# Chunks of 64 tokens in an mLSTM cell with a multiplicative FFN: cell products on 64x64 quarters of TensorE, with loads, gates and schedule rearranged to suit

## The chip, the cores and the metric

The kernel runs on one core of a Trainium2 chip. The metric is the device time of one execution in microseconds. Each kernel was executed at least four times and profiled once. Where a run was slow (over 1.5% above the fastest of its kernel) the ratios leave it out. The inputs and outputs are fp32, except for the FFN weights, which arrive as 64-bit floats and are converted on the chip.

## The reference

```python
# attention: batch 4, heads 8, tokens 768, head size 40
for t in range(S):
    m_new  = max(f[t] + m, i[t]);  f_s = exp(f[t] + m - m_new);  i_s = exp(i[t] - m_new);  m = m_new
    C = f_s * C + i_s * outer(v[t], k[t]);   n = f_s * n + i_s * k[t]
    y[t] = sigmoid(o[t]) * (C @ q[t]) / max(|n . q[t]|, 1)
# FFN on x = y reshaped to (3072 tokens, 320)
out = ((x @ w1) * (x @ w2)) @ w3 @ w_out          # d_ff = 1024
```

The recurrence is computed in chunks. Within a chunk a masked and weighted score matrix replaces the loop. Between chunks a state carries C and n. The kernel folds w3 @ w_out into one matrix (w3o) on the chip.

## The kernel before

A chunk is 128 tokens, and a unit is one chunk of one batch: 24 units. Each step of the main loop brings one unit through its stages, with pieces of FFN work in between, so that TensorE has something to do while other engines work for the cell. A cell has four products: ss (scores), ph (weighted scores times v), pi (state times q) and pc (what is added to the state). An FFN "up" makes 128 hidden columns for 512 tokens, a "down" the output of 128 tokens, and the "fold" is w3 @ w_out. The gate row of every head is written to DRAM once and read back into all 128 partitions (`pw`), exponentiated by ScalarE and masked by GpSimd.

```python
L = 128                                   # tokens of a chunk
def load_u(n):                            # the gate rows of unit n, in every partition
    u_t[n] = io.tile([L, H, L], FP, name="pw", tag="pw", bufs=4)
    nc.sync.dma_start(out=u_t[n], in_=U_d[c][b * H:(b + 1) * H, :].unsqueeze(0).to_broadcast([L, H, L]))
def scores(n):                            # two heads at once, in two halves of the rows
    for p in range(NP):
        for hip in range(2):
            r = slice(hip * DP, (hip + 1) * DP)
            nc.tensor.matmul(ss[hip][:, p, :], lhsT=kT[r, p, :], rhs=qT[r, p, :], start=True, stop=True)
    ...                                   # pw = ss * pw, on VectorE
def cell(n):
    ...   # pi: state times q, 4 matmuls of 82 columns;  h = pi * gT
    for hd in range(H):
        nc.tensor.matmul(ph[:, hd, :], lhsT=pw[:, hd, :], rhs=vt[:, hd, :], start=True, stop=True)   # 41 columns
    ...   # h += ph;  pc: k times weighted v, 4 matmuls of 82 columns;  state += pc
def ffn_up(gr, f):                        # pa, pb: 2 full products each, then the 64 remaining rows of both, side by side
    ...
```

Of the kernel before, what the change touches and what calls it, by code (L numbers as in the profile page):

```python
# [8 lines left out]
FP = mybir.dt.float32  # L9
# [6 lines left out]
def kernel(  # L16
# [27 lines left out]
    L = 128  # L44
    NT = S // L
    NU = B * NT
# [4 lines left out]
    BH = B * H  # L51
    DFF = moe_w1.shape[1]
    FO = DFF // L
    KF = DM // L
    REM = DM - KF * L
    GT = B
    TG = GT * L
# [16 lines left out]


    NB, NBQ = 4, 3
    qbuf = [const.tile([L, H, DP], FP, name=f"qbuf{i}") for i in range(NBQ)]
    kbuf = [const.tile([L, H, DP], FP, name=f"kbuf{i}") for i in range(NB)]
    vbuf = [const.tile([L, H, D1], FP, name=f"vbuf{i}") for i in range(NB)]
    ident = const.tile([128, 128], FP, name="ident")  # L80
    one = const.tile([BH, 1], FP, name="one")
    state = [const.tile([128, NP, 2, D1], FP, name=f"state{b}") for b in range(B)]
    aT = const.tile([L, NT, BH], FP, name="aT")
    gT = const.tile([L, NT, BH], FP, name="gT")
    wT = const.tile([L, NT, BH], FP, name="wT")
    decP = const.tile([128, B * NP, NT], FP, name="decP")
    U_d = [dram.tile([BH, L], FP, name=f"U_d{c}") for c in range(NT)]
# [3 lines left out]

    def load(n):
        c, b = divmod(n, B)
        for dst, src in ((qbuf[n % NBQ][:, :, 0:D], q), (kbuf[n % NB][:, :, 0:D], k), (vbuf[n % NB][:, :, 0:D], v)):
            nc.sync.dma_start(out=dst, in_=src[b, :, c * L:(c + 1) * L, :].rearrange("h p d -> p h d"))

    def load_o(c):
        o_t[c] = io.tile([L, B, H, D], FP, name="o_in", tag="o_in", bufs=2)
        for b in range(B):
            nc.sync.dma_start(out=o_t[c][:, b], in_=o_gate[b, :, c * L:(c + 1) * L, :].rearrange("h p d -> p h d"))  # L100

    def load_u(n):
        c, b = divmod(n, B)
        u_t[n] = io.tile([L, H, L], FP, name="pw", tag="pw", bufs=4)
        nc.sync.dma_start(out=u_t[n], in_=U_d[c][b * H:(b + 1) * H, :].unsqueeze(0).to_broadcast([L, H, L]))


    with tc.tile_pool(name="gates", bufs=1) as gates:
        f_sb = gates.tile([BH, S], FP, name="f_sb")
        a = gates.tile([BH, S], FP, name="a")  # L110
        nc.sync.dma_start(out=f_sb, in_=f_gate.rearrange("b h s -> (b h) s"))
        nc.sync.dma_start(out=a, in_=i_gate.rearrange("b h s -> (b h) s"))
        load(0)

        nc.vector.memset(one, 1.0)
        make_identity(nc, ident)
        for i in range(NB):
            nc.gpsimd.memset(kbuf[i][:, :, D:DP], 0.0)
            if i < NBQ:
                nc.gpsimd.memset(qbuf[i][:, :, D:DP], 0.0)  # L120
            nc.gpsimd.memset(vbuf[i][:, :, D:D1], 1.0)
        for t in state:
            nc.gpsimd.memset(t, 0.0)

        F = gates.tile([BH, S], FP, name="F")
        U = gates.tile([BH, S], FP, name="U")
        g, w = F, f_sb
        m0 = gates.tile([BH, NT], FP, name="m0")
        dec = gates.tile([BH, NT], FP, name="dec")

        def gate_cols(src, dst, c0, c1):
            pg = tps([L, c1 - c0, BH], "pg")
            for c in range(c0, c1):
                nc.tensor.transpose(pg[:, c - c0, :], src[:, c * L:(c + 1) * L], ident[0:BH, 0:BH])
            nc.vector.tensor_copy(out=dst[:, c0:c1, :], in_=pg)


        nc.vector.tensor_copy(out=f_sb[:, 0:1], in_=a[:, 0:1])
        for c0, c1 in ((0, 1), (1, NT)):
            rs = slice(c0 * L, c1 * L)  # L140
            for c in range(c0, c1):
                r = slice(c * L, (c + 1) * L)
                nc.vector.tensor_tensor_scan(out=F[:, r], data0=one.to_broadcast([BH, L]), data1=f_sb[:, r], initial=0.0,
                                             op0=OP.mult, op1=OP.add)
                if c > 0:
                    nc.vector.tensor_scalar(out=a[:, r], in0=a[:, r], scalar1=m0[:, c:c + 1], scalar2=None,
                                            op0=OP.subtract)
                nc.vector.tensor_tensor_scan(out=U[:, r], data0=f_sb[:, r], data1=a[:, r],
                                             initial=0.0 if c else -1.0e30, op0=OP.add, op1=OP.max)
                if c == 0:  # L150
                    nc.vector.tensor_copy(out=m0[:, 1:2], in_=U[:, L - 1:L])
                elif c < NT - 1:
                    nc.vector.tensor_tensor(out=m0[:, c + 1:c + 2], in0=m0[:, c:c + 1],
                                            in1=U[:, (c + 1) * L - 1:(c + 1) * L], op=OP.add)
            nc.vector.tensor_tensor(out=U[:, rs], in0=F[:, rs], in1=U[:, rs], op=OP.subtract)
            for c in range(c0, c1):
                nc.sync.dma_start(out=U_d[c], in_=U[:, c * L:(c + 1) * L])
            nc.vector.tensor_tensor(out=a[:, rs], in0=a[:, rs], in1=F[:, rs], op=OP.subtract)
            gate_cols(a, aT, c0, c1)
            if c0 == 0:  # L160
                for n in range(2):
                    load_u(n)
                load_o(0)
                load(1)
            U3, w3d, a3 = (x.rearrange("p (c t) -> p c t", t=L)[:, c0:c1] for x in (U, w, a))
            nc.vector.tensor_tensor(out=w3d, in0=a3, in1=U3[:, :, L - 1:L].to_broadcast([BH, c1 - c0, L]), op=OP.add)
            nc.scalar.activation(out=dec[:, c0:c1], in_=U3[:, :, L - 1], func=AF.Exp)
            nc.scalar.activation(out=g[:, rs], in_=U[:, rs], func=AF.Exp)
            nc.scalar.activation(out=w[:, rs], in_=w[:, rs], func=AF.Exp)
            gate_cols(w, wT, c0, c1)  # L170
            if c0 > 0:
                gate_cols(g, gT, c0, c1)


        nc.sync.dma_start(out=dec_d, in_=dec)
        for hip in range(2):
            nc.sync.dma_start(out=decP[hip * DP:(hip + 1) * DP],
                              in_=dec_d.rearrange("(n two) c -> two n c", two=2)[hip:hip + 1]
                              .to_broadcast([DP, B * NP, NT]))

    ffn = ctx.enter_context(tc.tile_pool(name="ffn", bufs=2))
# [7 lines left out]
    w3_t = {}  # L189
# [3 lines left out]
    def to_f32(dst, pieces):  # L193
# [3 lines left out]
        raw = wst.tile([128, n, 2], U32, name="raw", tag="raw", bufs=2)  # L197
        for rows, src in pieces:
            nc.sync.dma_start(out=raw[rows].rearrange("p n two -> p (n two)"), in_=src)
# [16 lines left out]
    every = slice(0, 128)  # L216

    def cvt_w12(half, i):
        c0 = half * CW
        if i < 2 * KF:  # L220
            dst, src = ((w1, w1_d), (w2, w2_d))[i // KF]
            ko = i % KF
            to_f32(dst[:, ko, c0:c0 + CW], [(every, src[ko * 128:(ko + 1) * 128, cols(c0, CW)])])
        else:
            to_f32(wr[:, c0:c0 + CW], [(slice(j * REM, (j + 1) * REM), src[KF * L:DM, cols(c0, CW)])
                                       for j, src in enumerate((w1_d, w2_d))])

    def cvt_wo(ko):
        to_f32(wo[:, ko, :], [(every, wo_d[ko * 128:(ko + 1) * 128, :])])

    def cvt_w3(ko):
        w3_t[ko] = wst.tile([128, DFF], FP, name="w3", tag="w3")
        for c0 in range(0, DFF, CW):
            to_f32(w3_t[ko][:, c0:c0 + CW], [(every, w3_d[ko * 128:(ko + 1) * 128, cols(c0, CW)])])
# [4 lines left out]
    def w3_trans(ko):  # L239
        w3 = w3_t.pop(ko)  # L240
        w3T_t[ko] = wst.tile([128, FO, 128], FP, name="w3T", tag="w3T")
        for half in range(2):
            tp = tps([128, FO // 2, 128], "w3p")
            for j in range(FO // 2):
                ki = half * (FO // 2) + j
                nc.tensor.transpose(tp[:, j, :], w3[:, ki * 128:(ki + 1) * 128], ident)
            r = slice(half * (FO // 2), (half + 1) * (FO // 2))
            if half:
                nc.scalar.copy(out=w3T_t[ko][:, r, :], in_=tp)
            else:  # L250
                nc.vector.tensor_copy(out=w3T_t[ko][:, r, :], in_=tp)  # L251
# [11 lines left out]
    def out_gate(c):  # L263
        nc.scalar.activation(out=o_t[c], in_=o_t[c], func=AF.Sigmoid)
# [194 lines left out]
```

## Time and profile before

| | before |
|---|---|
| median of 4 runs | 578.04 us (572.49 to 580.81) |
| span of the profiled run | 573.4 us |
| TensorE busy | 532.6 us, 93% |
| units arrive in steps 0 to 5 | every 5 to 13 us |
| step 20 (two ups, one down, a unit's whole cell) | 19.3 us |

The prediction below shows the shares, the stages and a unit's chain.

### The profile page before, as it was taken

Reading aid. Unit: us, or ns where it says so; the run is one execution under the profiler, and the core shown is the slowest. Engines: PE = TensorE matmul, PEld = TensorE weight load, DVE = VectorE, ACT = ScalarE, POOL = GpSimd, SP = SyncE. Lnnn points to the kernel's source line nnn. Section 1 sums busy time; section 2 is a strip of 40 time slices with the busy share of each in tenths; the row PEclk is TensorE's granted clock in tenths of the full one; section 3 lists DMA queues with packets and bytes.
Section 4 is the critical chain, followed back from the end, with each engine's and each line's share of the span. In section 5 each row is a group of like instructions: output and inputs, shape, how many; then the busy total and the mean of one; then the engine's idle time right before and its main releaser. Section 6 shows DMA issues by size and latency. Waiting matters only on the chain.

```text
span 573.4 us, 6858 instructions
## 1 busy us (share of the span) xinstructions
PE 532.6 (93%) x2521; PEld 339.2 (59%) x2521; DVE 256.7 (45%) x581; ACT 166.2 (29%) x377; POOL 72.6 (13%) x105
## 2 busy tenths in 40 slices
PE   0869899889698999999999999999999999999997
PEld 0759766546366566688886656565453353535375
DVE  7356989997978665765431332132001101010100
ACT  2745354534231314434553211111111111111100
POOL 2222322142011202122220100000000000000000
PEclk9985799989798998999999999999999999999999
DMA  7499986868353554334733200000000000000010
GB/s 163 71 202 225 212 185 156 181 164 201 97 170 111 144 127 114 97 72 108 152 95 95 59 13 11 13 7 5 23 24 1 0 24 0 23 1 23 0 35 34
DMA packets 114224, 49.28 MB, mean 86 GB/s; under 512 B 103440, under 2 KB 106704, under 8 KB 114192
## 3 DMA queue, kind: packets, MB, share of 16 engines
q1 hardware_dynamic: 114192, 48.85, 36.3%
q8 instruction: 20, 0.33, 0.2%
q14 instruction: 12, 0.10, 0.1%
HBM read 44.81 MB, written 4.03 MB: 85 GB/s over the span
## 4 chain that ended last, share of the span: by engine, by line
PE 78%; DVE 13%; DMA 4%; ACT 2%; SPq 1%; issue 1%; ACTq 0%; DVEq 0%
PE po L375 18%; PE pa L364 12%; PE pb L364 12%; PE pa L367 7%; PE wp L257 7%; PE ph L309 6%; PE pt L278 4%; PE ss L289 4%; PE pc L320 3%; PE pi L304 3%; DMA kbuf<-in_k_dram 2%; DMA raw<-in_moe_w_dram 2%; DVE pw L292 2%; DVE ex L208 2%; PE px L351 1%; DVE ma L210 1%
## 5 line engine op out<-in xcount | busy, mean ns | idle before, releaser
L370 DVE TENSOR_TENSOR ab<-pb,a_sb 128x512 f32<-128x512 f32 x48 | 33.2, 691 | 212.8 <-ACT a_sb L369 212.6
L375 PE MATMUL po<-w3o,ab 128*128 128x320 f32 x384 | 105.9, 433 | 0.0
L364 PE MATMUL pa<-xT,w 128*128 128x512 f32 x192 | 93.9, 610 | 0.5 <-ACT xT L352 0.5
L364 PE MATMUL pb<-xT,w 128*128 128x512 f32 x192 | 91.3, 597 | 0.0
L375 PEld LDWEIGHTS po<-w3o,ab 128*128 128x128 f32 x384 | 71.9, 190 | 31.4 <-issue 3.0
L369 ACT COPY a_sb<-pa 128x512 f32<-128x512 f32 x48 | 28.1, 585 | 187.4 <-PE pb L367 187.4
L270 ACT ACTIVATE pw<-pw,aT 128x128 f32<-128x128 f32 x192 | 60.1, 391 | 24.7 <-DMA pw<-U_d 24.6
L364 PEld LDWEIGHTS pb<-xT,w 128*128 128x128 f32 x192 | 36.6, 192 | 45.0 <-issue 44.7
L364 PEld LDWEIGHTS pa<-xT,w 128*128 128x128 f32 x192 | 33.2, 191 | 37.3 <-issue 34.9
L367 PE MATMUL pa<-xT,wr 64*128 64x512 f32 x96 | 53.9, 641 | 0.1
L367 PE MATMUL pb<-xT,wr 64*128 64x512 f32 x96 | 53.9, 641 | 0.0
L309 PE MATMUL ph<-vbuf,pw 128*128 128x41 f32 x384 | 50.9, 292 | 1.9 <-DVE pw L292 1.0
L309 PEld LDWEIGHTS ph<-vbuf,pw 128*128 128x128 f32 x384 | 48.8, 203 | 3.7 <-DVE pw L292 1.3
L257 PE MATMUL wp<-wo,w3T 128*128 128x320 f32 x128 | 40.8, 475 | 5.6 <-DVE w3T L251 5.5
L271 POOL TENSOR_SCALAR_AFFINE_SELECT pw<-pw 128x1024 f32<-128x1024 f32 x24 | 31.6, 1316 | 104.4 <-ACT pw L270 103.6
L292 DVE TENSOR_TENSOR pw<-ss,pw 128x512 f32<-128x512 f32 x48 | 30.9, 682 | 11.2 <-PE ss L289 11.1
L257 PEld LDWEIGHTS wp<-wo,w3T 128*128 128x128 f32 x128 | 26.0, 209 | 16.5 <-DVE w3T L251 6.2
L367 PEld LDWEIGHTS pa<-xT,wr 64*128 64x128 f32 x96 | 14.1, 184 | 36.5 <-issue 35.5
L289 PEld LDWEIGHTS ss<-qT,kT 64*128 64x128 f32 x384 | 28.2, 210 | 10.1 <-issue 6.2
L378 ACT COPY o_sb<-po 128x320 f32<-128x320 f32 x24 | 10.2, 425 | 78.3 <-PE po L375 75.5
L289 PE MATMUL ss<-qT,kT 64*128 64x128 f32 x384 | 30.9, 303 | 1.4 <-ACT qT L281 1.1
L320 PE MATMUL pc<-vw,kbuf 128*128 128x82 f32 x160 | 24.6, 302 | 0.1
(75 smaller groups left out, 520.3 us busy)
## 6 DMA issues: line engine op xcount, KB each, us to landing
pw<-U_d SPq DMA_DIRECT2D x24, 512.0 KB, 5.2
raw<-in_moe_w_dram SPq DMA_DIRECT2D x24, 512.0 KB, 4.0
qbuf<-in_q_dram SPq DMA_DIRECT2D x24, 160.0 KB, 4.2
kbuf<-in_k_dram SPq DMA_DIRECT2D x24, 160.0 KB, 3.9
vbuf<-in_v_dram SPq DMA_DIRECT2D x24, 160.0 KB, 3.9
o_in<-in_o_gate_dram SPq DMA_DIRECT2D x24, 160.0 KB, 3.8
out_dram<-o_sb SPq DMA_DIRECT2D x24, 160.0 KB, 1.8
raw<-in_moe_w_out_dram SPq DMA_DIRECT2D x8, 320.0 KB, 3.2
```

Source lines behind the costliest of these rows:

```text
L257: nc.tensor.matmul(wp, lhsT=w3T[:, ki, :], rhs=wo[:, ki, :], start=(ki == 0), stop=(ki == FO - 1))
L270: nc.scalar.activation(out=pw[:, h, :], in_=pw[:, h, :], func=AF.Exp, bias=aT[:, c, b * H + h:b * H + h + 1])
L271: nc.gpsimd.affine_select(out=pw, in_=pw, compare_op=OP.is_ge, fill=0.0, base=0, pattern=[[0, H], [1, L]], channel_multiplier=-1)
L289: nc.tensor.matmul(ss[hip][:, p, :], lhsT=kT[r, p, :], rhs=qT[r, p, :], start=True, stop=True)
L292: nc.vector.tensor_tensor(out=pv[:, :, hip, :], in0=ss[hip], in1=pv[:, :, hip, :], op=OP.mult)
L309: nc.tensor.matmul(ph[:, hd, :], lhsT=pw[:, hd, :], rhs=vt[:, hd, :], start=True, stop=True)
L320: nc.tensor.matmul(pc[:, p].rearrange("p a b -> p (a b)"), lhsT=kbuf[n % NB][:, 2 * p:2 * p + 2, :].rearrange("p a b -> p (a b)"), rhs=vw[ ...
L364: nc.tensor.matmul(p, lhsT=wt[:, cc, fs], rhs=x[:, cc, :], start=(cc == 0), stop=False)
L367: nc.tensor.matmul(p, lhsT=wr[r, fs], rhs=x[r, KF, :], start=False, stop=True)
L369: nc.scalar.copy(out=a_sb, in_=pa)
L370: nc.vector.tensor_tensor(out=ab_t[gr][:, f, :], in0=pb, in1=a_sb, op=OP.mult)
L375: nc.tensor.matmul(po, lhsT=ab_t[gr][:, f, j * L:(j + 1) * L], rhs=w3o[:, f, :], start=(f == 0), stop=(f == FO - 1))
```

## The change

The chunk becomes 64 tokens. A unit is now the same 64 tokens of two batches, so that it still fills 128 partitions. All cell products become matmuls of 64 rows by 64 columns, addressed to the four quarters of the array, four at a time (two for `ph`). The first weights are fetched right after the gate inputs. The gates of all later chunks are computed in one pass. FFN work starts two steps earlier, conversions go two pieces a step. The q, k, v and o loads become two half-unit transfers each, since the halves come from different batches.

```diff
-    L = 128
+    L = 64
...
     def load_u(n):
-        u_t[n] = io.tile([L, H, L], FP, name="pw", tag="pw", bufs=4)
-        nc.sync.dma_start(out=u_t[n], in_=U_d[c][b * H:(b + 1) * H, :].unsqueeze(0).to_broadcast([L, H, L]))
+        u_t[n] = io.tile([P, H, L], FP, name="pw", tag="pw", bufs=3)
+        src = (U_rest[c - 1] if c else U_first).rearrange("(two bp h) t -> bp two (h t)", two=2, bp=NB2)[bp]
+        nc.sync.dma_start(out=u_t[n].rearrange("p h t -> p (h t)"), in_=src.unsqueeze(1).to_broadcast([2, L, H * L]))
...
     def scores(n):
-            for hip in range(2):
-                r = slice(hip * DP, (hip + 1) * DP)
-                nc.tensor.matmul(ss[hip][:, p, :], lhsT=kT[r, p, :], rhs=qT[r, p, :], start=True, stop=True)
+            for hip, x in ((0, 0), (1, 1), (0, 1), (1, 0)):
+                r, t = halves[hip], halves[x]
+                nc.tensor.matmul(ss[t, hip, p, :], lhsT=kT[r, p, t], rhs=qT[r, p, t], start=True, stop=True)
...
     def cell(n):            # pi and pc likewise in four quarters, ph in the two diagonal ones
+            for r in halves:
+                nc.tensor.matmul(ph[r, hd, :], lhsT=pw[r, hd, :], rhs=vt[r, hd, :], start=True, stop=True)
...
-    n_up = [0] * 6 + [2] * 8 + [0] * 6 + [2] * 6 + [4] * 5 + [0]
-    n_down = [0] * 18 + [2, 2, 1, 1, 1, 1, 2, 2, 0, 2, 2, 2, 2, 4]
+    n_up = [0] * 4 + [4, 0, 3, 3, 3, 3] + [2] * 8 + [0] + [2] * 5 + [4, 2, 4, 4]
+    n_down = [0] * 18 + [4, 1, 1, 1, 1, 2, 2, 2, 2, 2, 2, 4]
+    n_cvt = [2, 1, 1, 1, 2, 2] + [2] * 12
```

## The prediction

> **What bounds the kernel now.** I read the page's busy shares and slices first, to see which engine limits which stretch; then a table of windows by stage; then the chain of waits in one steady step and the timeline around one change of array shape, because the change rewrites what TensorE does there.
>
> The slices of the page: each digit is the busy share of 1/40 of the span (14.3 us).
>
> ```profile
> PE 532.6 (93%) x2521; PEld 339.2 (59%) x2521; DVE 256.7 (45%) x581; ACT 166.2 (29%) x377; POOL 72.6 (13%) x105
> ...
> PE   0869899889698999999999999999999999999997
> ...
> DVE  7356989997978665765431332132001101010100
> ...
> PEclk9985799989798998999999999999999999999999
> ```
>
> TensorE is busy from slice 11 on without a gap, at full clock. Before that it has an empty first slice, a stretch at a lower clock (digits 5 and 7), and two dents (the 6s). VectorE is near 90% only in slices 5 to 12. The same by stage; columns are the stretch, its length, then busy us of TensorE, its weight loads, VectorE, ScalarE, GpSimd, then clock, DMA share and GB/s:
>
> ```profile
> 0.00:20.00 20.00, 5.69 (x31) 4.89 (x32) 10.92 (x35) 8.95 (x18) 5.81 (x24) 1.00 0.72 149
> 20.00:80.00 60.00, 50.44 (x312) 42.96 (x310) 42.38 (x89) 29.30 (x73) 14.64 (x18) 0.74 0.91 183
> 80.00:284.00 204.00, 190.38 (x1075) 130.18 (x1074) 154.73 (x358) 79.50 (x182) 43.12 (x49) 0.96 0.56 136
> 284.00:412.00 128.00, 128.00 (x634) 82.57 (x634) 33.98 (x78) 29.76 (x71) 8.99 (x15) 1.00 0.15 40
> 412.00:574.00 162.00, 158.12 (x477) 78.58 (x475) 14.73 (x22) 18.65 (x36) 0.00 (x0) 1.00 0.04 15
> ```
>
> From 20 to 80 us the DMA engines are 91% busy and the clock is 0.74: the first six units arrive at the pace of loads and conversions, and TensorE work saved there is mostly hidden. From 80 to 284 us TensorE loses 13.6 us, and from 284 us on it is the only limit: there each microsecond taken off it is a microsecond of the end.
>
> One steady unit in the chain (start, us, what):
>
> ```profile
> 316.22 0.89 PE ss L289 x16
> 317.11 1.05 PE pi L304 x8
> 318.16 1.75 PE ph L309 x16
> 319.92 0.93 PE pc L320 x8
> ```
>
> Each fp32 product is two instructions. The sixteen ss instructions run as eight pairs in two halves of the rows, 0.11 us a pair. The ph instructions have 41 columns, yet cost 1.75 / 16 = 0.109 us each: they are paced by loading 128 weight columns. One unit's products are 4.62 us.
>
> An FFN "up" is eight full streams of 0.43 us and two paired half-row ones, 4.30 us, but the chain repeats it every 4.69 us (443.20 to 447.89). The timeline shows where 0.39 us goes:
>
> ```profile
> 446.76 0.69 PE L367 MATMUL pa<-xT,wr 64*128 64x512 f32 x1
> 446.77 0.69 PE L367 MATMUL pb<-xT,wr 64*128 64x512 f32 x1
> ...
> 447.30 0.59 PE L367 MATMUL pa<-xT,wr 64*128 64x512 f32 x1
> ...
> 447.82 0.19 PEld L364 LDWEIGHTS pa<-xT,w 128*128 128x128 f32 x1 [0.76 <-issue]
> ```
>
> The last half-row stream starts at 447.30 and needs 0.43, so it is through at 447.73; the next load starts at 447.82, 0.09 us later, and its 0.11 us is not hidden either. A change of array shape thus costs about 0.20 us.
>
> **What the Trainium skill says.** "TensorEngine Tiling (Array Packing)", Key Properties: changing the tiling mode, not merely the tile, drains TensorE. The trace agrees: 0.09 us and an exposed weight load. "TensorE: Matmul & The Clock Gate", Part 3, Measured speedup vs the span model: four row tiles ran 3.07 times as fast, sixteen tiles 10.6 times, with some 4 ns per further tile, at 512 columns. The trace has only two row tiles, which start 5 to 10 ns apart and run fully side by side; no quarters. The same page, section LDWEIGHTS: loading takes the number of columns / 1.2 ns, 107 ns for 128; measured 0.109 to 0.112 in ph. Its Part 1 ("Wait — 56ns, not 53.3ns?") has a floor of about 25 ns from one matmul's start to the next. Nothing here is that dense (ss: 56 ns per matmul), so this trace cannot say whether the quarters meet it.
>
> **The change, part by part.**
>
> 1. Cell products. A unit is again 128 tokens (64 of two batches), so there are 24 still. With 12 chunks, pi and pc run in 22 units instead of 20. Each product of a unit is now 16 matmuls, 32 instructions, of 64 columns of weights: half of 0.112, 0.056 us, say 0.058. With four quarters side by side ss, pi and pc take 8 x 0.058 = 0.46 us each; ph uses only the two diagonal quarters, 16 x 0.058 = 0.93 us. After: 24 x 0.46 + 22 x 0.92 + 24 x 0.93 = 54 us. Before: 24 x 0.89 + 20 x 0.89 (pi without its shape change) + 24 x 1.75 + 20 x 0.93 = 100 us. Saved: 46 us of TensorE.
>
> 2. Shape changes. Walking through the compiled order of TensorE's instructions I count 121 changes of shape before and 246 after: the scheduler lays pi, ph and pc between full-array matmuls (pa, pi, pa, pc, pb), where formerly all but ss and the remainder rows were full array. Into full or half-row shape 0.20 us, into quarters 0.09 + 0.06 = 0.15 us: 24 us before, 46 us after. Added: 21 us.
>
> 3. Gate transposes become 140 small matmul instructions instead of 17: some 6 us more, at the start, where TensorE waits anyway; I count 2.
>
> 4. Transposes, the up and down products and the weight fold stay in columns. The first group's ups are split in two halves (their further shape changes are in point 2), so that FFN work starts two steps earlier, in step 4. Replacing each piece by its duration gives a warm, gapless TensorE of 505 us before and 487 us after. The first figure leaves 68 us of the present span to waiting and the low clock.
>
> 5. Start and conversions. Broadcast gate rows are half as large (24 x 256 KB less), one weight conversion is moved into the gate phase and conversions go two pieces a step, with three raw buffers. Formerly TensorE idled before the first fold: the chain shows a weight transfer from 136.75 to 143.57 us, then conversions to 152.71. I expect 10 us of that stretch back. The first ph at 23.55 us should come about 3 us sooner; it can't be more, as the scheduler puts the 704-column scans ahead of the first chunk's.
>
> 6. What lies beside other work. Six of 24 units fall in the DMA- and VectorE-paced start, so of 46 us some 35 reach the end; of the 21 us of shape changes, about 20 do, being mostly in later steps. Earlier ups fill some 5 us of the idle start.
>
> Sum: 576 - 35 + 20 + 2 - 10 - 3 - 5 = 545 us.
>
> **Rivals.**
>
> *Quarters run only two at a time.* For: the old trace shows pairs in different rows only, and two quarters of one row half need different moving data. Then ss, pi and pc cost 0.93 each, 31 us more TensorE, some 23 on the path: 568. If ph's diagonal quarters, which write the same bank, also serialise, another 17: 585.
>
> *Instruction rate.* A product is 64 TensorE instructions. At 25 ns for each, loads too, it takes 1.6 us and the 92 products 147 us, 47 more than now, plus the shape changes: 630 or above. If only matmuls are so spaced, 0.8 us a product: 562. Against: pairs in ss start within 10 ns, so a filled queue issues fast.
>
> *One buffer for ss, pi and pc.* They now share one two-bank PSUM tile: ss, VectorE's mask product (two of 0.68 us, now one), pi, the h product (0.49), pc, the state sum follow each other strictly, some 5 us a step with handovers. A late step has 19 us of TensorE work to hide it; early steps, where VectorE also has two conversions (up to 7.5 us), don't. This could put back my 10 to 15 us of start: 555 to 560.
>
> *Everything fits and the clock holds:* 520.
>
> **Range and chances.** I give full quarters with modest waits a half, two-at-a-time or a matmul floor a third, worse the rest. Centre 545, range 518 to 576. The 2% line is 565. Faster 0.76: the full-quarter and best rivals and half the middle ones. Same 0.14, slower 0.10 for the instruction rate.
>
> **What would show it.** Right: in late steps ss and pc take about half a microsecond in the chain, ph 0.9; matmuls of four quarters start within 30 ns; gaps of 0.1 us at each shape change; TensorE remains without gaps after 290 us; the first downs come before 300 us though half of the ups are then done. Wrong: ss at 0.9 or more (no four-way overlap), ph at 1.8, TensorE waiting for VectorE before pi or pc, a low clock far beyond 80 us, or a hole left before the first fold.

## More of the kernel before

A group's columns are line, engine, operation, tiles, shapes and count, then busy us and mean ns, then the engine's idle time before it and what ended that; a transfer's are tiles, queue, count, size and the median time to landing.

```profile
L309 PE MATMUL ph<-vbuf,pw 128*128 128x41 f32 x384 | 50.9, 292 | 1.9 <-DVE pw L292 1.0
...
L270 ACT ACTIVATE pw<-pw,aT 128x128 f32<-128x128 f32 x192 | 60.1, 391 | 24.7 <-DMA pw<-U_d 24.6
...
pw<-U_d SPq DMA_DIRECT2D x24, 512.0 KB, 5.2
```

The first is the cell product with the most TensorE time for the least arithmetic: 41 columns behind each load of 128 weight columns. The second says that ScalarE waited 24.6 us in all for gate rows (10.3 more stand before loads of its function table on the same line). They took 5.2 us to land, but these waits cost TensorE nothing that shows: the chain of the work that ended last has no gate row in it.

## The result

| | before | changed |
|---|---|---|
| median | 578.04 us (4 runs) | 611.72 us (610.15 to 614.07, 4 runs) |
| ratio | | 1.060, 95% interval 1.051 to 1.069 |
| TensorE busy in the profiled run | 532.6 us | 524.4 us |
| first ss of unit 18 | 284.3 us | 361.9 us |

A ratio here is always the mean time of one kernel's fast runs over that of the other's fast runs of the same rounds, so it isn't quite the ratio of the medians. The changed kernel is 6% slower. The prediction had 545 us, and 518 to 576 as its range: the direction was wrong.

The page of the changed kernel: busy shares, then the slices (15.2 us each).

```profile
PE 524.4 (86%) x4596; PEld 315.9 (52%) x4596; DVE 239.9 (39%) x538; ACT 156.4 (26%) x409; POOL 80.3 (13%) x134
...
PE   3654776999797898698977969999999999999997
...
DVE  7436476677856673443722311212332210010000
...
PEclk9999796599979999989989869999999999999999
```

TensorE does less work than before and is idle longer. The idle time is no longer confined to the start: there are digits of 6 to 8 up to slice 23, some 360 us. VectorE, which the prediction's rivals suspected, isn't at 90% in any slice. By stage (start and end, length, then busy us of TensorE, weight loads, VectorE, ScalarE, GpSimd, then clock, DMA share, GB/s):

```profile
0.00:20.00 20.00, 4.69 (x48) 3.41 (x48) 15.78 (x34) 4.74 (x10) 4.90 (x20) 1.00 0.57 129
20.00:80.00 60.00, 38.92 (x623) 32.02 (x624) 29.82 (x68) 20.24 (x58) 14.58 (x20) 0.94 0.64 120
80.00:284.00 204.00, 174.62 (x1833) 108.36 (x1833) 128.65 (x301) 68.31 (x178) 37.74 (x55) 0.91 0.53 118
284.00:412.00 128.00, 113.03 (x1084) 66.42 (x1085) 36.95 (x80) 33.27 (x91) 17.14 (x28) 0.92 0.22 44
412.00:608.00 196.00, 193.13 (x1010) 105.71 (x1010) 28.70 (x57) 29.82 (x74) 5.97 (x12) 1.00 0.06 20
```

From 20 to 80 us TensorE now loses 21 us (9.6 before), from 80 to 284 us 29 us (13.6 before), from 284 to 412 us 15 us (none before). And the DMA share fell from 0.91 to 0.64 between 20 and 80 us: the DMA engines as a whole have more room, so it isn't a lack of bandwidth.

A late unit, where TensorE is still the limit, in the chain of the changed kernel:

```profile
389.07 0.62 PE ss L243 x32
389.69 0.90 PE ph L266 x32
...
391.65 0.61 PE pi L259 x32
...
393.31 0.61 PE pc L278 x32
```

This is what the prediction had asked for: about 0.6 for ss, pi and pc with their change of shape, 0.90 for ph. In the trace's single records the four quarters start 6.7 ns apart and a group of four follows the last after 58.5 ns; the 32 instructions of ss start within 0.48 us. So the quarters deliver, and the time must be lost elsewhere. The page's chain of waits says where, by engine and by line:

```profile
PE 66%; DMA 16%; SPq 7%; DVE 4%; ACT 4%; issue 2%; POOL 0%; ACTq 0%; DVEq 0%; POOLq 0%
PE po L436 17%; PE pb L423 12%; DMA pw<-U_rest 12%; PE pa L423 11%; PE pa L426 7%; PE wp L210 6%; SPq L109 3%; PE ph L266 3%; ACT pw L223 2%; PE pi L259 2%; SPq L116 2%; DMA raw<-in_moe_w_dram 2%; PE ss L243 2%; PE pt L232 1%; PE pc L278 1%
```

One transfer, the broadcast of the gate rows, makes 12% of the span: some 73 us. SPq, which is SyncE issuing transfers, makes 7%. Before, the first was not on the list and the second was 1%:

```profile
PE 78%; DVE 13%; DMA 4%; ACT 2%; SPq 1%; issue 1%; ACTq 0%; DVEq 0%
PE po L375 18%; PE pa L364 12%; PE pb L364 12%; PE pa L367 7%; PE wp L257 7%; PE ph L309 6%; PE pt L278 4%; PE ss L289 4%; PE pc L320 3%; PE pi L304 3%; DMA kbuf<-in_k_dram 2%; DMA raw<-in_moe_w_dram 2%; DVE pw L292 2%; DVE ex L208 2%; PE px L351 1%; DVE ma L210 1%
```

The list of waits (who waited for what: us in total, times, longest) has the engine that was held up, first before, then in the changed kernel:

```profile
ACT pw L270 <- DMA pw<-U_d: 24.6, 14, 5.3
...
ACT L270 <- DMA pw<-U_d: 10.3, 2, 7.5
```

```profile
ACT pw L223 <- DMA pw<-U_rest: 81.4, 11, 10.2
...
ACT L223 <- DMA pw<-U_rest: 32.6, 4, 9.7
```

And the chain around one such wait shows how a late transfer for ScalarE becomes TensorE's loss (start, us, what):

```profile
223.71 0.94 PE ph L266 x32
...
224.79 7.62 DMA pw<-U_rest
...
233.00 1.52 ACT pw L223 x6
234.53 0.48 ACT a_sb L428
...
235.05 1.98 PE pb L423 x4
```

The transfer starts when ph has freed a gate buffer and needs 7.6 us, for half as many bytes as the one that needed 5.2 us before. Behind the exponentials of this gate row ScalarE's list has the copy of an FFN product out of PSUM, the memory that TensorE writes to (`a_sb`). The last product into that buffer starts at 229.53; the copy starts at 234.43, right after the exponentials, and TensorE stands idle for 1.86 us before its next product, which needs the buffer, starts at 235.05. So TensorE stops until the gate row of a later unit has landed and been worked on.

Why 7.6 us? In the records of the packets, the 128 packets of 2 KB of one broadcast take 93 ns each on average and are spread over 5.2 to 6.6 us. 128 x 0.093 / 6.0 = 2.0: two engines at work, of sixteen. The Trainium skill has the rule, in "DMA: Bandwidth & Descriptors", section "Why a DMA increments its semaphore by 16 and not by 1": the number of engines is the largest one up to 16 that divides the slowest dimension, other than 1, of both access patterns. The new source's slowest dimension is 2 (the two batches); the old one's was 128. The prediction does not draw on this page.

### The profile page after: what moved, and what is told of

Same layout as the page of the kernel before. It is cut to its first block, busy times and chain, and to the rows that moved or that the text cites. A ratio compares the mean times of both kernels' runs of the same rounds, so it can differ in the third digit from the quotient of the medians.

```text
span 608.5 us, 11187 instructions
## 1 busy us (share of the span) xinstructions
PE 524.4 (86%) x4596; PEld 315.9 (52%) x4596; DVE 239.9 (39%) x538; ACT 156.4 (26%) x409; POOL 80.3 (13%) x134
## 4 chain that ended last, share of the span: by engine, by line
PE 66%; DMA 16%; SPq 7%; DVE 4%; ACT 4%; issue 2%; POOL 0%; ACTq 0%; DVEq 0%; POOLq 0%
PE po L436 17%; PE pb L423 12%; DMA pw<-U_rest 12%; PE pa L423 11%; PE pa L426 7%; PE wp L210 6%; SPq L109 3%; PE ph L266 3%; ACT pw L223 2%; PE pi L259 2%; SPq L116 2%; DMA raw<-in_moe_w_dram 2%; PE ss L243 2%; PE pt L232 1%; PE pc L278 1%
## 5 line engine op out<-in xcount | busy, mean ns | idle before, releaser
L431 DVE TENSOR_TENSOR ab<-pb,a_sb 128x512 f32<-128x512 f32 (+1 forms) x56 | 34.3, 613 | 253.4 <-ACT a_sb L428 234.1
L423 PE MATMUL pb<-xT,w 128*128 128x512 f32 (+1 forms) x224 | 101.4, 574 | 18.4 <-ACT a_sb L428 15.5
L423 PE MATMUL pa<-xT,w 128*128 128x512 f32 (+1 forms) x224 | 103.3, 575 | 9.5 <-ACT xT L310 9.5
L223 ACT ACTIVATE pw<-pw,aT 128x64 f32<-128x64 f32 x192 | 49.3, 336 | 88.5 <-DMA pw<-U_rest 81.4
L428 ACT COPY a_sb<-pa 128x512 f32<-128x512 f32 (+1 forms) x56 | 29.1, 519 | 148.9 <-PE pb L426 135.1
L426 PE MATMUL pa<-xT,wr 64*128 64x512 f32 (+1 forms) x112 | 58.2, 603 | 0.5 <-DVE wr L154 0.5
L426 PE MATMUL pb<-xT,wr 64*128 64x512 f32 (+1 forms) x112 | 58.5, 604 | 0.0
L225 POOL TENSOR_SCALAR_AFFINE_SELECT pw<-pw 64x512 f32<-64x512 f32 x48 | 32.3, 673 | 113.8 <-ACT pw L223 112.1
L266 PE MATMUL ph<-vbuf,pw 64*64 64x41 f32 x768 | 32.7, 241 | 6.1 <-ACT xT L310 6.1
L266 PEld LDWEIGHTS ph<-vbuf,pw 64*64 64x64 f32 x768 | 29.8, 151 | 8.6 <-ACT xT L310 6.3
L210 PEld LDWEIGHTS wp<-wo,w3T 128*128 128x128 f32 x128 | 24.7, 199 | 11.6 <-DVE w3T L204 2.1
L232 PE MATMUL pt<-ident,qbuf 128*128 128x128 f32 x96 | 17.1, 306 | 11.6 <-DMA qbuf<-in_q_dram 11.6
```

The costliest lines, as they stand in the source:

```text
L210: nc.tensor.matmul(wp, lhsT=w3T[:, ki, :], rhs=wo[:, ki, :], start=(ki == 0), stop=(ki == FO - 1))
L223: nc.scalar.activation(out=pw[:, h, :], in_=pw[:, h, :], func=AF.Exp, bias=aT[:, c, bp * H + h:bp * H + h + 1])
L225: nc.gpsimd.affine_select(out=pw[r], in_=pw[r], compare_op=OP.is_ge, fill=0.0, base=0, pattern=[[0, H], [1, L]], channel_multiplier=-1)
L232: nc.tensor.transpose(pt[:, p, :], src[:, 2 * p:2 * p + 2, :].rearrange("p a b -> p (a b)"), ident)
L266: nc.tensor.matmul(ph[r, hd, :], lhsT=pw[r, hd, :], rhs=vt[r, hd, :], start=True, stop=True)
L423: nc.tensor.matmul(p, lhsT=wt[:, cc, fs], rhs=pick(x[:, cc, :]), start=(cc == 0), stop=False)
```

## The experiments

The theories were: **A**, the broadcast is served by two engines; **B**, there are three gate buffers now where there were four, so that it starts too late; **C**, SyncE's issuing of twice as many transfers is the bound (from 20 to 120 us the trace shows it issuing for 90% of the time; the 94% in the first expectation was misread). Ten kernels ran, and all gave correct results. Each is compared with runs of the kernel before in its own rounds.

### 1. The broadcast as two transfers

```diff
-        nc.sync.dma_start(out=u_t[n].rearrange("p h t -> p (h t)"), in_=src.unsqueeze(1).to_broadcast([2, L, H * L]))
+        for x in range(2): nc.sync.dma_start(out=u_t[n][halves[x]].rearrange("p h t -> p (h t)"), in_=src[x:x + 1].to_broadcast([L, H * L]))
```

> Changed kernel with each unit's gate broadcast issued as two transfers of 64 partitions, so that no access pattern has a slowest dimension of 2. Theory A (a transfer whose slowest dimension is 2 is served by two DMA engines: 128 packets took 6 us, sum of packet time over elapsed time is 2.0): landing falls from 8 to some 2.5 us, the waits of ScalarE for it (81 + 33 us) nearly vanish, time 612 -> 545 to 570. Theory B (three gate buffers instead of four: the load starts a step too late): landing matters little, 595 to 610. Theory C (SyncE's issue time: it is 94% busy issuing in the first 120 us, twice as many transfers as before): 22 more issues, 612 to 625.

Measured: 562.30 us (559.93 to 563.42), ratio to before 0.973 (0.967 to 0.979). The same packets, both halves together, are now spread over 1.6 to 3.2 us. Another count agrees, if each engine that takes part in a transfer ends its share with one 4-byte packet: 24 broadcasts on two engines turned into 48 on sixteen would add 48 x 16 - 24 x 2 = 720, and the records have 4945 such packets where the changed kernel has 4225. The waits of ScalarE and the page's line of the transfer (size and median landing of each half):

```profile
ACT pw L223 <- DMA pw<-U_rest: 30.0, 6, 5.8
ACT L223 <- DMA pw<-U_rest: 10.6, 2, 5.6
```

```profile
pw<-U_rest SPq DMA_DIRECT2D x44, 128.0 KB, 3.2
```

The waits fall from 114 to 41 us in all, not to almost nothing, and the time falls by 49 us, from 6% slower to 2.7% faster. One line made the whole difference in sign. Theory C expected this run, with more issues, to be no faster, and is out as a cause of its own. But SyncE's time is part of the damage: with 309 issues instead of 285 it is busy issuing for 190 us in all instead of 234, and its part of the chain falls from 7% to 3%:

```profile
PE 78%; DVE 8%; DMA 6%; SPq 3%; issue 2%; ACT 1%; POOL 1%; DVEq 0%; ACTq 0%; POOLq 0%
```

So the slow broadcast also held up the issuing of other transfers; by what way, the trace doesn't show.

### 2. Four gate buffers, the broadcast as it was

```diff
-        u_t[n] = io.tile([P, H, L], FP, name="pw", tag="pw", bufs=3)
+        u_t[n] = io.tile([P, H, L], FP, name="pw", tag="pw", bufs=4)
```

> Changed kernel with four gate buffers as before, the broadcast left as it is. Theory A: a transfer of 8 us may start a step earlier; late steps gain part, the start (where the two engines are busy for 6 of every 12 us) little: 585 to 605. Theory B: 545 to 570. Theory C: 608 to 615.

Measured: 619.71 us, ratio 1.072 (1.065 to 1.079). Theory B is out: a fourth buffer alone is no help. But all three expectations were missed, A's too: the run is no faster than the changed kernel (1.060, 1.051 to 1.069, in other rounds). ScalarE still waits 74 + 21 us for gate rows. The chain has less of the broadcast (8% instead of 12%) and more of SyncE's issuing (10% instead of 7%) and of the weights' transfers (5% instead of 2%): the time moved on to the next transfers. Why it came to as much was not tested; the scheduler also moved instructions.

### 3. Both edits

> Both edits. Theory A: within 1% of the first run (545 to 570), the fourth buffer adds nothing. Theory B: like the second run. If the two are of the same size and add: 530 to 550.

Measured: 556.81 us (555.96 to 560.92), ratio 0.966 (0.960 to 0.971). With the transfers fast, the fourth buffer is worth some 5 us at most: the ranges of runs 1 and 3 overlap (559.93 to 563.42 and 555.96 to 560.92). ScalarE's waits for gate rows are down to 22 us. TensorE's busy time is 504.8 us, 28 less than before.

### 4. The two-engine broadcast in the kernel before

```diff
-    U_d = [dram.tile([BH, L], FP, name=f"U_d{c}") for c in range(NT)]
+    U_d = [dram.tile([2, BH, L], FP, name=f"U_d{c}") for c in range(NT)]
-        nc.sync.dma_start(out=u_t[n], in_=U_d[c][b * H:(b + 1) * H, :].unsqueeze(0).to_broadcast([L, H, L]))
+        nc.sync.dma_start(out=u_t[n].rearrange("p h t -> p (h t)"), in_=U_d[c][:, b * H:(b + 1) * H, :].rearrange("two h t -> two (h t)").unsqueeze(1).to_broadcast([2, L // 2, H * L]))
-                nc.sync.dma_start(out=U_d[c], in_=U[:, c * L:(c + 1) * L])
+                for two in range(2): nc.sync.dma_start(out=U_d[c][two], in_=U[:, c * L:(c + 1) * L])
```

> Kernel of before, with the gate rows stored twice and the broadcast read as 2 x 64 rows of 4 KB, so that its source's slowest dimension is 2; the copies land the same bytes. Theory A: 128 packets at 0.16 us over two engines make 10 us a unit, 24 x 10 = 245 us; the first six units, which come every 10 us now, come every 12 to 14: 578 -> 600 to 625. Theories B and C: within 5 us of before.

Measured: 759.98 us (758.41 to 763.33), ratio 1.317 (1.310 to 1.324). The shape of one access pattern, with the same bytes landing in the same places, costs the old kernel 32%. The direction was expected, the size was not. The packets of one broadcast are spread over some 10.6 to 12.2 us, about the 10 us worked out, but the loss is not confined to the first units. The chain by line:

```profile
DMA pw<-U_d 14%; DMA raw<-in_moe_w_dram 12%; PE po L375 11%; PE pa L364 7%; PE pb L364 7%; PE ph L309 5%; SPq L100 4%; PE pa L367 4%; PE wp L257 4%; SPq L95 4%; PE ss L289 2%; ACT pw L270 2%; PE pi L304 2%; PE pc L320 2%; DMA raw<-in_moe_w_out_dram 2%
```

The weights' transfers, untouched by the edit, now hold 12% of the span (2% before), and issuing a k load takes SyncE 2.63 us on average instead of 0.54. ScalarE's waits for gate rows grow from 35 to 241 us. If the broadcast makes two of the sixteen engines slow, and a transfer over all sixteen has to wait for these two, both readings would follow; the records don't name the engine of a packet, so it's an argument and not shown.

### 5. A control for the order of instructions

Run 1 changed the scheduler's order as well. This kernel has run 1's two transfers per unit, and in the traces TensorE, VectorE, ScalarE and GpSimd run the same instructions in the same order as in run 1. But it stores the rows twice, so that the slowest dimension is 2 once more.

```diff
-    U_rest = dram.tile([NT - 1, BH, L], FP, name="U_rest")
+    U_rest = dram.tile([2, NT - 1, BH, L], FP, name="U_rest")
-        for x in range(2): nc.sync.dma_start(out=u_t[n][halves[x]].rearrange("p h t -> p (h t)"), in_=src[x:x + 1].to_broadcast([L, H * L]))
+        for x in range(2): nc.sync.dma_start(out=u_t[n][halves[x]].rearrange("p h t -> p (h t)"), in_=src[x].unsqueeze(1).to_broadcast([2, L // 2, H * L]))
```

(Against run 1. U_first and the line of `src` likewise, and both stores are issued twice.)

> Control for the first run, whose scheduler also reordered instructions: the same two transfers per unit and nearly the same order (ScalarE's identical), but the gate rows are stored twice, so that each transfer reads 2 x 32 rows and its source's slowest dimension is 2 again. If the engines per transfer are the cause: back to 600 to 620. If the new order was: about 562.

Measured: 630.14 us (626.98 to 632.73), ratio 1.095 (1.086 to 1.103), above even the expected range. A broadcast's packets are spread over 6.5 to 8.7 us again, and the waits are back:

```profile
ACT pw L223 <- DMA pw<-U_rest: 97.1, 12, 10.7
ACT L223 <- DMA pw<-U_rest: 43.9, 6, 11.6
```

So the new order was not what helped run 1. The 4-byte packets fit two engines in runs 4 and 5 as well (2817 and 4305, the doubled stores counted with sixteen each). Theory A stands on three runs: taking the shape away, putting it into the other kernel, and putting it back.

### 6 and 7. SyncE's issuing in what is left

```diff
-        for x in range(2):
-            nc.sync.dma_start(out=o_t[gr][halves[x], j], in_=rows(o_gate, n, x))
+        for x in range(2 if n % NB2 == 0 else 0):
+            nc.sync.dma_start(out=o_t[gr][halves[x], j:j + NB2], in_=o_gate[x * NB2:(x + 1) * NB2, :, n // NB2 * L:(n // NB2 + 1) * L, :].rearrange("b h p d -> p b h d"))
```

This is on top of run 3; run 7 issues the same transfers from GpSimd (`nc.gpsimd.dma_start`).

> The third run (both edits, 557) with the output-gate loads of two units joined: 24 transfers of 128 descriptors' rows more instead of 48. Theory C' (what is left of the slow start is SyncE's issuing, 17 to 19 of every 20 us up to 60 us): some 0.6 us less issuing a unit, the first six steps shrink by 2 to 5 us together: 550 to 555. If issuing is hidden: 555 to 559.

> The same with these joined loads issued by GpSimd (14% busy) and not by SyncE. Theory C': a further 0.7 us a unit off SyncE, 546 to 554. If issuing is hidden, or GpSimd's own issuing is in its way: 555 to 562.

Measured: 559.41 us (0.971, 0.966 to 0.977) and 554.66 us (0.965, 0.958 to 0.972), against run 3's 0.966 (0.960 to 0.971) in other rounds. Neither differs from run 3 by more than the noise: both medians lie above the range expected if issuing were the limit. Joining the loads shortened the first six steps by 0.7 us together, not by 2 to 5. So issuing is not what limits the repaired kernel, although SyncE is at it for up to 19 of 20 us early on.

### 8. Conversions earlier

```diff
-    n_cvt = [2, 1, 1, 1, 2, 2] + [2] * 12
+    n_cvt = [2, 1, 1, 1, 2, 2, 3, 3, 3] + [2] * 7 + [1, 0]
```

> The third run with three weight conversions instead of two in steps 6 to 8, so that the first fold's two pieces are converted a step and a half earlier. The step before the first fold takes 29.0 us against 19.7 for those after it. If that hole is conversion work that starts too late: 548 to 553. If TensorE just runs out of matrix work earlier instead: 554 to 560.

Measured, on top of run 3: 553.08 us (552.49 to 553.22), ratio 0.961 (0.956 to 0.966); run 3's interval, from other rounds, overlaps it. The median is at the upper edge of "starts too late" (548 to 553), but the profile doesn't bear the reason out. The fold comes sooner, and the long step moves with it (26.6 us, now step 8 instead of 10). TensorE's wait there is larger than in run 3 (4.3 us):

```profile
PE w3p L199 <- DVE w L154: 9.0, 1, 9.0
```

The steps after it are shorter, 18.8 instead of 19.7 us, but that only makes up for it: unit 17 begins at 295.3 us (294.4 in run 3). The gain, 3.6 us at unit 18, is that of step 17, which has no conversion left (11.6 instead of 16.1 us). Why the others are shorter was not separated.

### 9. Two PSUM buffers for ss, pi and pc

Shortened to the numbers of buffers:

```diff
-    ps_t = ... bufs=3 ...   ps_s = ... bufs=1 ...   ps_m = ... bufs=3 ...
+    ps_t = ... bufs=2 ...   ps_s = ... bufs=2 ...   ps_m = ... bufs=2 ...
```

> The third run with two instead of one two-bank PSUM buffers for ss, pi and pc, taken from the other two pools (3 -> 2 each). The rival of the prediction, that the one shared buffer chains ss, mask product, pi, h, pc and state sum: TensorE waits 12 us before pi and 14 us before pc for VectorE; if they come from the shared buffer they shrink by more than half and the time, unless the smaller pools cost as much, is 545 to 552. If the buffer is no bound (VectorE is late for its own work), the loss of a buffer in each other pool shows: 558 to 575.

Measured, on top of run 3: 570.06 us (569.83 to 571.25), ratio 0.988 (0.983 to 0.993). The run is mixed and settles the rival only in part. The waits of TensorE before pi and pc for VectorE, 12 and 14 us in run 3, are gone from the top of its list, so the shared buffer did cause them. But the buffers had to come from the FFN's and the transposes' pools, and that costs more. In their place stand waits like this one:

```profile
PE pa L423 <- ACT a_sb L428: 7.1, 13, 0.7
```

All eight banks are in use, so the shared buffer could not be doubled without that price.

### 10. All that seemed to help, together

Run 7 with the conversions of run 8.

> The version meant to beat both: two-part broadcast, four gate buffers, joined output-gate loads from GpSimd, conversions earlier. If the gains of the last two add: 548 to 553; if both only fill the same idle stretch: 552 to 556.

Measured: 562.39 us (559.05 to 567.88, 6 runs, one of them slow), ratio 0.976 (0.969 to 0.983), which leaves open whether it is 2% faster than before. Both expected ranges were missed. The two don't add: together they are slower than run 8, and than run 7 by medians (the intervals overlap a little). The long step of the fold is 27.1 us again and the one after it 24.7. The lowest median is therefore run 8's: 553.08 us, 3.9% faster than before, and 9.6% below the changed kernel's median. From runs 3 and 7 it is not told apart by the ratios.

## Why the prediction was wrong

**The step that failed** is the one the prediction put as "Broadcast gate rows are half as large (24 x 256 KB less)", under point 5. It counted the bytes of the new transfer and not the shape of its access pattern, took half the bytes for less time, and so had no rival in which this transfer becomes the wait. Measured: 128 packets over 6 us on two engines where 16 would do, 7.6 to 8.6 us to landing in the chain, 114 us of ScalarE's waiting instead of 35. Through ScalarE's order this goes on to TensorE. Behind it SyncE's issuing grew in the chain too (41 us, 8 before). Repairing this one line takes 49 us off (run 1). Of the prediction's own signs of being wrong, three came: "a low clock far beyond 80 us" (0.91 and 0.92 until 412 us, in the stretches with TensorE's gaps), TensorE waiting for VectorE before pi or pc (19 us in all) and "a hole left before the first fold". None names a transfer.

**Point 1, the products,** was right in size: ss, pi and pc 0.61 to 0.62 us with a shape change of 0.15 in it (0.46 had been worked out), ph 0.90 (0.93). The rivals of two quarters at a time and of a slow instruction rate did not occur. The second could have been lowered beforehand: the prediction says that its trace cannot tell about the floor of 25 ns, but the pairs of ss in that same trace start 6 to 7 ns apart.

**Point 2, the shape changes,** was right where it can be read: the traces have the 121 and 246 changes that were counted, and from the last half-row stream, which starts at 388.48 and takes 0.43, to the first quarter load at 389.00 there is 0.09 us. A late step with two ups, one down and a whole cell takes 17.98 us, 19.31 before. The four products are 1.88 us less (4.62 to 2.74, the changes into quarters included), so that some 0.55 us goes on the further changes back to full shape, three at about 0.20 as expected.

**Points 1 to 4 together,** a warm gapless TensorE 18 us shorter: with the broadcast repaired and four gate buffers (run 3), TensorE's busy time is 28 us less and the span 18 us less than before. The busy time is not the gapless time of the prediction, so this agrees in kind only. (Its reading that TensorE is gapless and at full clock "from slice 11 on" was too early: its own table shows 13.6 us lost up to 284 us, and slices 12 and 15 have a clock digit of 8.)

**Point 5, the start and the fold,** failed in its other terms too. The first ph came at 30.5 us (27.1 in run 3) instead of 3 us before 23.55. The step of the first fold takes 29.0 us in run 3 and 27.7 us before, so that none of the 10 us came back, and the first down starts at 311.6 us in run 3, not before 300. These two terms are 13 of the 31 us that the prediction's sum takes off 576; without them it gives 558, and run 3 measured 557. That the two match is in part luck: in run 3 the first ph is not only not earlier but 3.5 us later than before, so some other term was better than predicted.

**The rival of one PSUM buffer** was real: some 25 us of TensorE's waiting in run 3. What these waits cost stays open, as run 9 shows no net gain by this remedy.

**What stays open:** how the slow broadcast holds up SyncE and other transfers, why the step of the first fold is long (in all of these kernels but run 7, where steps 9 and 10 take 20.9 and 19.9 us), why run 2 gains nothing, and why runs 7 and 8 don't add.

## What to carry to other kernels

When a transfer's shape is rewritten, work out how many DMA engines will serve it before counting its bytes: a new outer dimension of 2, here the two halves of the partitions, left it on two engines. Here one transfer for each half put it right. Check in the trace that packet time over elapsed time isn't stuck near that dimension: it was 2.0 here, and 5 to 10 after the repair. A slow transfer is paid for by whatever stands behind its reader in the engine's list, which may be work for somebody else, as ScalarE's copy for TensorE was here.

## What the Trainium skill lacked or had wrong

- "DMA: Bandwidth & Descriptors", section "Why a DMA increments its semaphore by 16 and not by 1", is right on the engine count (2.0 engines measured for a slowest dimension of 2). It doesn't say what such a transfer does to others issued with it: in run 4 the issue of an untouched load by SyncE rose from 0.54 to 2.63 us on average, and the kernel by 32%.
- "TensorEngine Tiling (Array Packing)", Key Properties, says that a change of mode drains, but gives no time. Here it is 0.09 to 0.10 us, with the next weight load no longer hidden (0.11 us for 128 columns).
- "TensorE: Matmul & The Clock Gate", Part 1, has a floor of about 25 ns from one matmul's start to the next and doesn't say there that it is one for matmuls on the same part of the array. Across four quarters it does not hold: they start 6.7 ns apart, and the 32 fp32 instructions of ss start within 0.48 us, 15 ns each, with their weight loads in between. Part 3 of the page, as the prediction cites it, is nearer.
